# Smaller conversion steps, earlier loads, another order of the second sweep and four more quarters of h loaded ahead, in a retention and mixture-of-experts kernel

## The chip, the cores and the metric

The kernel runs on one core of a Trainium2 chip. The metric is the device time of one execution in microseconds (us). The engines are TensorE (PE in the profile), VectorE (DVE), ScalarE (ACT), GpSimd (POOL) and SyncE (SP), which here only issues DMAs. Each engine works through its instructions in the order in which they were written, and waits for others by semaphores.

## The reference

All tensors are float32. First a retention layer runs over q, k and v of shape (4 batches, 8 heads, 768 positions, 64):

```python
for t in range(S):
    state = gamma * state + einsum('bhd,bhe->bhde', k[:, :, t], v[:, :, t])
    y[:, :, t] = scale * einsum('bhd,bhde->bhe', q[:, :, t], state)
```

Its output, as x of shape (3072 tokens, 512), goes through a mixture of 8 experts with 1024 hidden features, weighted by P, which comes from 8 Sinkhorn iterations:

```python
P = exp(x @ w_gate - max)
for _ in range(8):
    P /= P.sum(1, keepdims=True) + 1e-09
    P /= P.sum(0, keepdims=True) + 1e-09
    P *= N / E
for e in range(E):
    out += P[:, e:e + 1] * (maximum(x @ w1[e], 0) @ w2[e])
```

## The kernel before

**Precision.** PE takes its operands in a reduced float32 form. Every operand is split into a high part (rounded by ACT, `hi_act`, L77) and a low part (the difference, by DVE or POOL, `lo`, L80), and every product is made of three matmuls: high by high, low by high, high by low.

**Seven products.** Both expert layers multiply 2 x 2 blocks with seven products, M1 to M7, instead of eight. This needs sums and differences of blocks: of x (`x_tasks`, L128, through the scratch tile XSC), of w1 (`w1_tasks`, POOL adds at L158), of h, and of w2. A tile of x, `X0` or `X1`, has seven operands, each with a high slot and a low slot of 1024 columns; `XP` says which operand stands where.

**Attention.** 24 turns `tau`, each a chunk of 128 positions of one batch. In a turn: `loads(tau + 3)` puts the raw q, k and v of a later chunk on SP's queue; `split_qk(tau + 2)` makes high and low parts (kh, QH on ACT, kl on POOL, QL on DVE); `scores(tau + 1)`, `logits(tau - 1)`, `attend(tau)` and `state` work on PE, with evictions on DVE, and POOL scales keys (tk) and decays the state. `attend` stores the chunk of x to `xd` in HBM. From turn 8 on, tasks in the list `todo` are run two to a turn: the 22 steps that make X0 for the first third of the tokens (r = 0), and the conversion of the first two blocks of w1.

**First layer (UA).** 96 units, one for each pair of a block j of w1 (32 blocks of 256 hidden features) and a third r of the tokens. A unit is seven products of six matmuls each. `ROW` sets the order of seven groups: group m = 0 is M6 of unit n, m = 1 is M1 of unit n + 1, then M3 and M7 of n, M2 and M5 of n + 1, and M4 of n. `post` evicts each product by ACT or DVE, and SP stores seven parts of h to `hd`. M1, M6, M7 and M4 accumulate one upon the other in a PSUM bank, M5 and M3 in another, so a product waits for the eviction of the one before it. `order` sets which unit follows which: units 0 to 31 are all blocks with r = 0 (the first sweep); then r = 1 and r = 2 (the second sweep), in which a block is used for both. A job is one conversion of a block; three buffers `WA` hold converted blocks, and the raw tile `RW` holds two raw blocks. r = 0 and r = 2 use X0, r = 1 uses X1. Between groups, `run(wq, 1)` starts one task of w1, and `run(xq, ...)` one or two steps of x. At the end of units 12 to 30 one step of Sinkhorn (`sink`) follows.

**Second layer (UB).** 24 units, one for each pair of an expert and a third of the tokens, of 28 parts each. A part `s` is a quarter of one product, 6 matmuls. The raw quarter of h (later its low part) lies at `place(s)`, the high part in the ring `HH`. Quarters are loaded by `h_load` into a ring `HL` of 15 places in the three WA buffers, as these come free at the end of the first layer; quarters 8 to 11 lie in the slots of M1 in X0 instead (`HX`). `h_conv` makes high and low parts, five parts ahead. The first parts are worked in between the groups of the last unit of the first layer, the rest after it.

## Time and profile before

| what | value |
|---|---|
| median of 3 runs | 2055.17 us (2054.22 to 2057.34) |
| profiled execution | 2053.89 us |
| its span in the trace | 2051.8 us |
| mean granted clock of PE in it | 0.987 |
| PE busy | 1985.9 us, 97% of the span |
| DVE busy | 1527.7 us, 74% |
| ACT busy | 1041.7 us, 51% |
| POOL busy | 406.0 us, 20% |
| moved by DMA | 504.13 MB, 246 GB/s on average |

The profile is one execution, by the hardware profiler. A row of the timeline has the start and the duration in us, the engine, the line of the kernel, the operation, what it writes and reads, a count, and in brackets the idle time of the engine before it with what ended it. Matmul ends are modelled, so start times are the better measure for PE. A row of the busy times by stage gives, for a stretch of the span, its length, the busy time of each engine with its number of instructions, the clock granted to PE (1.00 is full), the busy share of the DMA engines and GB/s. A row of groups gives line, engine, operation and shapes, count, busy time and mean ns of one, and the idle time before with its main releasers.

### The profile page before, as it was taken

What the parts mean: (1) busy time and instruction counts of PE and PEld (TensorE: products, weight loads), DVE (VectorE), ACT (ScalarE), POOL (GpSimd) and SP (SyncE); (2) the same over time, 40 slices, a digit from 0 to 9 for tenths busy, and PEclk for the clock granted to TensorE, in tenths of its full rate; (3) what the DMA queues carried; (4) which work ended last, traced back from release to release, by engine and by line L of the source; (5) the groups of instructions that cost most, each with busy time, mean ns of one, the idle gap of its engine ahead of it and who ended that gap; (6) DMA issues with size and microseconds to landing.
All of it is one profiled execution on the core that took longest, in us unless ns stands there. A gap on an engine that the chain in (4) does not pass through costs nothing.

```text
span 2051.8 us, 28824 instructions
## 1 busy us (share of the span) xinstructions
PE 1985.9 (97%) x9273; PEld 1647.2 (80%) x9273; DVE 1527.7 (74%) x2083; ACT 1041.7 (51%) x1668; POOL 406.0 (20%) x422
## 2 busy tenths in 40 slices
PE   7797999998899999999999999999999999999998
PEld 7786887887688888888887788888888888888887
DVE  6795988995666666666677787878778777868766
ACT  3343564554444444444444565655555555655553
POOL 5462342341211121121123000100100101001001
PEclk9899999999999999999999999999999999999999
DMA  7755776776466666666667888998999999999997
GB/s 240 239 180 163 242 245 206 244 244 217 165 233 214 218 228 217 221 218 223 220 229 263 297 286 281 278 288 277 285 283 278 267 291 270 291 292 269 271 269 184
DMA packets 253191, 504.13 MB, mean 246 GB/s; under 512 B 27824, under 2 KB 40432, under 8 KB 250992
## 3 DMA queue, kind: packets, MB, share of 16 engines
q1 hardware_dynamic: 241088, 458.78, 66.3%
q0 software_dynamic: 11952, 43.52, 11.0%
q8 instruction: 72, 1.18, 0.2%
q14 instruction: 79, 0.65, 0.1%
HBM read 269.31 MB, written 232.88 MB: 245 GB/s over the span
## 4 chain that ended last, share of the span: by engine, by line
PE 90%; DVE 4%; DMA 3%; issue 1%; ACT 1%; SPq 1%; POOL 0%; DVEq 0%; ACTq 0%
PE psA L190 42%; PE psA L551 25%; PE psB L551 19%; DMA raw<-kT 1%; DVE QL L80 1%; PE ps_s L327 1%; PE ps_x L363 1%; DMA RW<-w 1%; PE psA L372 1%; PE ps_x L358 0%; PE ps_t L339 0%; DVE X L80 0%; DVE ta L330 0%; SPq L112 0%; DMA hd<-OT 0%
## 5 line engine op out<-in xcount | busy, mean ns | idle before, releaser
L190 PE MATMUL psA<-X,WA 128*128 128x512 f32 x4032 | 931.4, 393 | 24.1 <-DVE OT L213 18.8
L190 PEld LDWEIGHTS psA<-X,WA 128*128 128x128 f32 x4032 | 760.8, 189 | 190.2 <-DVE OT L213 20.9
L77 ACT ACTIVATE WA<-WA 128x512 fp32r<-128x512 f32 x668 | 403.1, 629 | 259.3 <-PE psB L551 116.7
L551 PE MATMUL psA<-WA,X 128*128 128x512 f32 x2296 | 531.4, 389 | 0.2 <-DVE XSC L562 0.2
L551 PEld LDWEIGHTS psA<-WA,X 128*128 128x128 f32 x2296 | 431.0, 188 | 89.9 <-issue 0.6
L551 PE MATMUL psB<-WA,X 128*128 128x512 f32 x1728 | 404.3, 390 | 5.1 <-ACT WA L77 3.1
L80 DVE TENSOR_TENSOR WA<-WA,WA 128x512 fp32r<-128x512 f32 x487 | 313.7, 685 | 99.4 <-ACT WA L77 94.9
L551 PEld LDWEIGHTS psB<-WA,X 128*128 128x128 f32 x1728 | 324.6, 188 | 74.8 <-ACT WA L77 4.2
L158 POOL TENSOR_TENSOR RW<-RW 128x256 f32<-128x256 f32 x244 | 220.8, 915 | 637.9 <-DMA RW<-w 412.8
L219 ACT ACTIVATE OT<-OT 128x512 f32<-128x512 f32 x96 | 60.7, 632 | 243.3 <-DVE OT L218 243.3
L80 DVE TENSOR_TENSOR WA<-RW,WA 128x768 fp32r<-128x768 f32 x122 | 142.5, 1169 | 54.0 <-ACT WA L77 53.9
L569 POOL DMA_DIRECT2D out<-XSC x56 | 48.5, 865 | 611.7 <-DVE XSC L564 365.6
L80 DVE TENSOR_TENSOR WA<-WA 128x512 fp32r<-128x512 f32 x181 | 121.7, 697 | 35.4 <-ACT WA L77 34.4
L213 DVE TENSOR_TENSOR OT<-psA,OT 128x512 f32<-128x512 f32 x96 | 66.2, 689 | 106.2 <-PE psA L190 106.2
L77 ACT ACTIVATE WA<-RW 128x768 fp32r<-128x768 f32 x122 | 109.4, 946 | 23.6 <-POOL RW L158 13.9
L225 DVE TENSOR_TENSOR OT<-psA,OT 128x512 f32<-128x512 f32 x96 | 66.2, 690 | 58.5 <-ACT OT L219 51.3
L229 ACT ACTIVATE OT<-psA 128x512 f32<-128x512 f32 x96 | 57.5, 599 | 77.1 <-PE psA L190 40.3
L236 DVE TENSOR_TENSOR OT<-OT 128x512 f32<-128x512 f32 x96 | 92.2, 961 | 3.3
L579 ACT ACTIVATE OT<-psA 128x512 f32<-128x512 f32 x96 | 57.4, 598 | 72.7 <-PE psA L551 68.8
L226 ACT ACTIVATE OT<-OT 128x512 f32<-128x512 f32 x96 | 60.7, 633 | 65.4 <-DVE OT L225 65.3
L240 DVE TENSOR_TENSOR OT<-OT 128x512 f32<-128x512 f32 x96 | 70.1, 730 | 30.0 <-ACT OT L229 26.1
L211 ACT ACTIVATE OT<-psA 128x512 f32<-128x512 f32 x96 | 57.4, 598 | 64.0 <-PE psA L190 63.9
(116 smaller groups left out, 1486.4 us busy)
## 6 DMA issues: line engine op xcount, KB each, us to landing
hd<-OT SPq DMA_DIRECT2D x672, 256.0 KB, 2.6
WA<-hd SPq DMA_DIRECT2D x668, 256.0 KB, 6.1
RW<-w SPq DMA_DIRECT2D x61, 512.0 KB, 4.5
out<-XSC POOLq DMA_DIRECT2D x56, 512.0 KB, 8.3
RW<-w SPq DMA_DIRECT2D x16, 1024.0 KB, 7.7
out<-OT POOLq DMA_DIRECT2D x27, 512.0 KB, 8.4
OT<-pd SPq DMA_DIRECT2D x23, 512.0 KB, 6.2
raw<-kT SPq DMA_DIRECT2D x24, 256.0 KB, 4.0
```

Of the source, the lines that this page charges most:

```text
L77: act.activation(o, i, AF.Copy)
L80: eng.tensor_tensor(o, full, rd(h), ALU.subtract)
L158: eng_add.tensor_tensor(x[:, WP[o]], x[:, WP[p]], x[:, WP[q]], op)
L190: pe.matmul(ps, w[:, a, k * P:(k + 1) * P], x[:, b, k * 512:(k + 1) * 512], start=i in PRE and k == 0 and m == 0, stop=k == 1 and m == 2, ...
L213: dve.tensor_tensor(c12, ps, u2, ALU.add)
L219: act.activation(o, o, AF.Relu)
L225: dve.tensor_tensor(o, ps, s1, ALU.add)
L226: act.activation(o, o, AF.Relu)
L229: act.activation(self.new("A12"), ps, AF.Relu)
L236: dve.tensor_tensor(t["S2"], t["S1"], t["A11"], ALU.subtract)
L240: dve.tensor_tensor(self.new("S4"), self.t["A12"], self.t["S2"], ALU.subtract)
L551: pe.matmul(ps[d] if isinstance(ps, tuple) else ps[:, d, :], w[:, a, q * 256 + d * P:q * 256 + d * P + P], h[b], start=i in PRE and q == 0 ...
```

## The change

Five things are changed.

1. **Steps of x.** `x_tasks` still has 22 steps, but each now holds one DVE operation (a difference, or a low part) and at most one rounding on ACT, and a low part comes four steps or so after its rounding. Before, a rounding and its low part were one step. The loads of `x_load` can be issued by halves, and come in another order.
2. **Tasks of w1.** The adds on POOL and the roundings on ACT become two tasks, so a job has four tasks, run in groups 0, 3, 5 and 6 (before: three, in groups 0, 1 and 5). Sinkhorn's maximum becomes three steps and its exponential three steps of up to six operations; they run at the ends of units 14 to 35, the last one (the transpose of P) at unit 38.
3. **Earlier loads.** Half of X0's loads are issued at turn 5 of attention, the other half at turn 8, after the loads of w1 jobs 0 and 1, whose tasks now come first in `todo`, in pairs; `todo` starts at turn 10. Jobs 2 and 3 are loaded at turn 16 (before: job 2 after attention, behind the loads of X1). The steps of X1 start in unit 1 instead of 0.
4. **Order of the second sweep.** Before: blocks 29, 30, 31 for r = 1, then for r = 2, then block after block. Now: 29, 30, 31 for r = 1; 28, 27, 26 for r = 1 and then r = 2; 29, 30, 31 again, converted a second time, for r = 2; then block after block. So there are 64 jobs instead of 61, and six units with r = 1 ahead of the first with r = 2. The reload of X0 stays at unit 32, its steps start in unit 33, five to a unit, with one low part in three on POOL.
5. **Quarters of h.** `HX` has eight places, in the slots of M1 and M2 of X0, instead of four. In the last unit of the first layer twelve quarters are loaded instead of eight, after it quarters 16 to 22 instead of 12 to 18.

The diff, without the exponential's operations, which are only put in a list:

```diff
-    def x_load(t, r):
-        for i, c, d in ((M1, 0, 0), (M7, 1, 0), (M3, 1, 1), (M2, 0, 1)):
-            for k in range(2):
+    def x_load(t, r, which=(0, 1)):
+        for i, c, d in ((M1, 0, 0), (M2, 0, 1), (M7, 1, 0), (M3, 1, 1)):
+            for k in range(2) if c in which else ():
...
     def x_tasks(t, engs):
...
-            tt(M5, b12, src(M1))
-            tt(M6, src(M3), src(M5))
-            tt(M7, src(M3), b12)
-            tt(M4, src(M2), src(M6))
-            for i in (M1, M5, M2, M6, M7, M3, M4):
-                one(i)
+            def step(n, w=w, src=src):
+                b12 = rd(w(M7))
+                hi = [M1, M2, M5, M6, M7, M3, M4][n] if n < 7 else None
+                if n < 4:
+                    o, a, b = [(M5, b12, src(M1)), (M6, src(M3), src(M5)), (M7, src(M3), b12), (M4, src(M2), src(M6))][n]
+                    dve.tensor_tensor(XSC[:, sc[o], :], a, b, ALU.subtract)
+                else:
+                    i = [M1, M5, M2, M6, M7, M3, M4][n - 4]
+                    lo(engs[n % len(engs)], w(i, 1), src(i), w(i, 0))
+                if hi is not None:
+                    hi_act(w(hi, 0), src(hi))
+
+            q += [lambda n=n, step=step: step(n) for n in range(11)]
...
             tt(M7, M1, M7, ALU.subtract)
+
+        def rounded():
             hi_act(a[:, 0:3, 0, :], x[:, 0:3, :])
             hi_act(a[:, 3:7, 0, :], x[:, 3:7, :])
...
-        return [adds, lambda: rest(slice(0, 3)), lambda: rest(slice(3, 7))]
+        return [adds, rounded, lambda: rest(slice(0, 3)), lambda: rest(slice(3, 7))]
...
-    for g in [[NJ - 3, NJ - 2, NJ - 1]] + [[j] for j in range(NJ - 4, 2, -1)] + [[2, 1, 0]]:
-        order += [(j if j >= NJ - 3 else 2 * NJ - 4 - j, j, r) for r in (1, 2) for j in g]
+    order += [(j, j, 1) for j in (NJ - 3, NJ - 2, NJ - 1)]
+    order += [(NJ + k, NJ - 4 - k, r) for r in (1, 2) for k in range(3)]
+    order += [(NJ + 3 + k, NJ - 3 + k, 2) for k in range(3)]
+    for g in [[j] for j in range(NJ - 7, 2, -1)] + [[2, 1, 0]]:
+        order += [(2 * NJ - 1 - j, j, r) for r in (1, 2) for j in g]
...
+                if tau == B + 1:
+                    x_load(X0, 0, (0,))
                 if tau == 2 * B:
-                    x_load(X0, 0)
                     w1_load(0)
                     w1_load(1)
-                    todo += x_tasks(X0, [dve]) + w1_tasks(0, pool, dve) + w1_tasks(1, pool, dve)
-                if tau > 2 * B:
+                    todo += [f for g in zip(w1_tasks(0, pool, dve), w1_tasks(1, pool, dve)) for f in g]
+                    x_load(X0, 0, (1,))
+                    todo += x_tasks(X0, [dve])
+                if tau > 2 * B + 1:
                     run(todo, 2)
+                if tau == 4 * B:
+                    w1_load(2)
+                    w1_load(3)
...
-        sink = [sink_max, sink_exp] + [sink_a, sink_b] * SINKHORN + [sink_t]
+        sop = sink_exp()
+        sink = [sink_max, sink_max2, sink_max3]
+        sink += [lambda k=k: run(sop, 6) for k in range(3)]
+        sink += [sink_a, sink_b] * SINKHORN + [sink_t]
...
-        HX = [X0[:, XP[M1], k // 2, (k % 2) * 512:(k % 2 + 1) * 512] for k in range(4)]
+        HX = [X0[:, XP[i], k // 2, (k % 2) * 512:(k % 2 + 1) * 512] for i in (M1, M2) for k in range(4)]
 
         def place(s):
-            return HX[s - 8] if 8 <= s < 12 else HL[(s if s < 8 else s - 4) % NHL]
+            return HX[s - 8] if 8 <= s < 16 else HL[(s if s < 8 else s - 8) % NHL]
...
         x_load(X1, 1)
-        wq = []
-        xq = x_tasks(X1, [dve])
-        w1_load(2)
+        wq, xq = [], []
         loaded = conv = 2
...
-        loaded = 3
+        loaded = 4
...
+            if n == 1:
+                xq = x_tasks(X1, [dve])
             if n == NJ:
                 x_load(X0, 2)
-                xq = x_tasks(X0, [dve, pool])
+            if n == NJ + 1:
+                xq = x_tasks(X0, [dve, dve, pool])
...
-                for s in (range(4) if n == NUA - 2 else range(4, 12)):
+                for s in (range(4) if n == NUA - 2 else range(4, 16)):
...
-                if m in (0, 1, 5):
+                if m in (0, 3, 5, 6):
                     run(wq, 1)
-                if m in (1, 6) or n >= NJ:
-                    run(xq, 2 if n >= NJ else 1)
+                if m in (1, 6) or n >= NJ and m in (0, 3, 5):
+                    run(xq, 1)
...
-            if 12 <= n < 12 + len(sink):
-                sink[n - 12]()
+            if 14 <= n < 13 + len(sink):
+                sink[n - 14]()
+            if n == 38:
+                sink[-1]()
...
-        for s in range(12, NHL + 4):
+        for s in range(16, NHL + 8):
             h_load(s)
```

More of the change, by code (lines that the diff above doesn't have):

```diff
@@ L117, in x_tasks @@
         sc = {M7: 0, M5: 1, M6: 2, M4: 3}
-        e = [engs[k % len(engs)] for k in range(22)]
         for k in range(2):
@@ L459, in sink_exp @@
             dve.tensor_copy(mx, ps[:, 0:1])
+        def sink_exp():
             x, n, r, q = [et[:, i, :] for i in range(4)]
             s1, s2 = [ei[:, i, :].bitcast(mybir.dt.int32) for i in range(2)]
[L462 to L466 removed]
@@ L475, in sink_exp @@
-            p2 = Pm.rearrange("p a b -> p (a b)")
-            dve.scalar_tensor_tensor(q, q, 1.0, s1.bitcast(F32), ALU.add, ALU.mult)
-            dve.tensor_tensor(p2, q, s2.bitcast(F32), ALU.mult)
+            l2, p2 = [t.rearrange("p a b -> p (a b)") for t in (L, Pm)]
+            ops = [
+                lambda: dve.tensor_scalar(x, l2, mx, -104.0, ALU.subtract, ALU.max),
+                lambda: dve.tensor_scalar(n, x, LOG2E, MAGIC, ALU.mult, ALU.add),
+                lambda: dve.tensor_scalar(n, n, MAGIC, None, ALU.subtract),
+                lambda: dve.scalar_tensor_tensor(r, n, -LN2_HI, x, ALU.mult, ALU.add),
+                lambda: dve.scalar_tensor_tensor(r, n, -LN2_LO, r, ALU.mult, ALU.add),
+                lambda: dve.tensor_scalar(x, n, -126.0, None, ALU.max),
+                lambda: dve.tensor_tensor(n, n, x, ALU.subtract),
+                lambda: dve.tensor_scalar(s1, x, 127.0, 8388608.0, ALU.add, ALU.mult),
+                lambda: dve.tensor_scalar(s2, n, 127.0, 8388608.0, ALU.add, ALU.mult),
+                lambda: dve.tensor_scalar(q, r, EXPC[0], None, ALU.mult),
+            ]
@@ L479, in sink_a @@
+            ops += [lambda c=c: dve.scalar_tensor_tensor(q, q, c, r, ALU.add, ALU.mult) for c in EXPC[1:]]
+            ops += [
+                lambda: dve.scalar_tensor_tensor(q, q, 1.0, s1.bitcast(F32), ALU.add, ALU.mult),
+                lambda: dve.tensor_tensor(p2, q, s2.bitcast(F32), ALU.mult),
+            ]
+            return ops
         def sink_a():
```

32 lines of the change are left out of this document (5 added, 27 removed).

## The prediction

> **What bounds the kernel now.** I read the page's busy shares first, then the chain of waits, then the busy time by stage, and last PE's timeline where a stage is not dense.
>
> ```profile
> span 2051.8 us, 28824 instructions
> PE 1985.9 (97%) x9273; PEld 1647.2 (80%) x9273; DVE 1527.7 (74%) x2083; ACT 1041.7 (51%) x1668; POOL 406.0 (20%) x422
> ```
> ```profile
> 537.53 571.94 PE psA L190 x2520
> ...
> 1142.38 5.44 PE psA L551 x24
> ```
>
> PE sets the end, so only time in which PE stands still, or runs at half clock, can be won. The chain gives the dense price: 571.94 / 2520 = 0.227 us for one matmul of 512 columns, 42 x 0.227 = 9.53 us for one unit of the first layer; 5.44 / 24 is the same price in the second layer. The stages by windows:
>
> ```profile
> core 0: us, PE busy (x) PEld busy (x) DVE busy (x) ACT busy (x) POOL busy (x), PEclk, DMA share, GB/s
> 63.70:96.20 32.50, 22.22 (x175) 20.92 (x173) 18.58 (x29) 8.83 (x16) 12.00 (x10) 0.74 0.73 235
> 96.20:166.30 70.10, 63.05 (x572) 57.47 (x571) 63.54 (x92) 25.59 (x41) 38.29 (x32) 0.95 0.51 163
> 166.30:222.20 55.90, 47.73 (x192) 37.69 (x192) 35.16 (x43) 23.95 (x39) 19.02 (x20) 0.94 0.65 207
> ...
> 332.70:500.30 167.60, 167.60 (x741) 138.37 (x740) 141.27 (x216) 86.49 (x136) 50.98 (x56) 0.99 0.71 234
> ...
> 507.00:537.50 30.50, 18.09 (x60) 13.21 (x60) 22.39 (x24) 12.59 (x24) 15.96 (x11) 0.83 0.39 125
> 537.50:1109.50 572.00, 571.96 (x2521) 472.58 (x2521) 369.03 (x482) 267.94 (x425) 110.65 (x122) 1.00 0.64 222
> 1109.50:1136.40 26.90, 21.77 (x85) 16.30 (x85) 21.43 (x23) 12.45 (x23) 12.52 (x8) 0.94 0.97 324
> 1136.40:2045.00 908.60, 908.40 (x4005) 751.85 (x4006) 708.89 (x981) 517.92 (x829) 71.74 (x83) 1.00 0.92 276
> ```
>
> From 537.5 to 1109.5 and from 1136.4 to 2045 PE is full at clock 1.00: nothing is to be had there. What is loose lies in five places: 63.7 to 166.3 (attention), 166.3 to 222.2 (start of the first sweep), around 310 to 330 (the first Sinkhorn steps), 507 to 537.5 (start of the second sweep over x) and 1109.5 to 1136.4 (the change of layers). PE's timeline names the waits:
>
> ```profile
> 166.28 11.18 PE L190 MATMUL psA<-X,WA 128*128 128x512 f32 x48 [0.45 <-DVE L L435]
> 182.96 11.15 PE L190 MATMUL psA<-X,WA 128*128 128x512 f32 x42 [5.50 <-DVE OT L213]
> 196.47 25.47 PE L190 MATMUL psA<-X,WA 128*128 128x512 f32 x102 [2.35 <-DVE OT L213]
> 222.25 85.43 PE L190 MATMUL psA<-X,WA 128*128 128x512 f32 x372 [0.31 <-ACT OT L229]
> 309.89 0.27 PE L453 MATMUL pmx<-ident,mx 128*1 128x128 f32 x1 [2.22 <-DVE mx L451]
> ...
> 329.98 15.38 PE L190 MATMUL psA<-X,WA 128*128 128x512 f32 x54 [2.88 <-DVE OT L213]
> ...
> 512.89 6.25 PE L190 MATMUL psA<-X,WA 128*128 128x512 f32 x18 [5.89 <-DVE OT L213]
> 521.70 5.73 PE L190 MATMUL psA<-X,WA 128*128 128x512 f32 x24 [2.55 <-ACT OT L229]
> ```
>
> **Part 1, start of the first sweep.** From 166.28 to 222.25 there are 48 + 42 + 102 = 192 matmuls, 43.6 us dense, in 56.0 us: 12.4 us are lost. PE names DVE L213, an eviction, but what DVE and ACT were held by is the raw W:
>
> ```profile
> 178.79 0.84 ACT L77 ACTIVATE WA<-RW 128x768 fp32r<-128x768 f32 x1 [6.14 <-DMA RW<-w]
> ...
> 192.85 0.85 ACT L77 ACTIVATE WA<-RW 128x768 fp32r<-128x768 f32 x1 [3.48 <-DMA RW<-w]
> ```
>
> Jobs 2 and 3 of W are loaded only after attention, job 2 behind the eight loads of X1 on SP. The change issues both at turn 16 of attention, eight turns ahead, and lets later jobs follow a unit earlier; it also moves X1's steps from unit 0 to unit 1. Both waits (5.50 and 2.35) and what the lower clock (0.94) took with them should go. The adds on POOL and the rounding on ACT become separate tasks, so ACT no longer stands behind POOL. I keep 2 us for a first unit that is not smooth: gain 10.5, bounds 7.8 (the two waits alone) to 12.4.
>
> **Part 2, first Sinkhorn steps.** The maximum, its transpose and 17 exponent steps now come in six units instead of two, at most 6 small DVE operations each, and each PE step finds its DVE operand a unit old. The waits of 2.22 and 2.88 go: gain 5, bounds 2.2 (only the transpose) to 7 (with the tails of both).
>
> **Part 3, start of the second sweep over x.** From 507 to 537.5 PE does 60 matmuls, 13.6 us dense: 16.9 us lost. X0 cannot be reloaded before its last use, and then 22 steps run at two to a matmul group while DVE waits for the loads with evictions behind it:
>
> ```profile
> 511.00 1.23 DVE L128 TENSOR_TENSOR XSC<-X,XSC 128x512 f32<-128x512 f32 x1 [1.66 <-DMA X<-xd]
> ```
>
> Six units on X1 now stand in front of the first on the new X0 instead of three, the steps begin one unit after the load and come at five a unit, ending in unit 37 before that unit's second group needs them. What is late next is DVE. Its base is the row of 332.7 to 500.3: 141.27 / 167.6 x 9.53 = 8.0 us a unit, W conversion and Sinkhorn included (they now reach to unit 35). Units 33, 34 and 35 add 5, 3 and 5 DVE operations of the x steps (the other two lo steps of unit 34 are POOL's); the price of one:
>
> ```profile
> 187.57 0.68 DVE L128 TENSOR_TENSOR XSC<-X,XSC 128x512 f32<-128x512 f32 x1
> ...
> 192.96 8.04 POOL L158 TENSOR_TENSOR RW<-RW 128x256 f32<-128x256 f32 x8 [10.07 <-DMA RW<-w]
> ...
> 194.60 1.21 DVE L128 TENSOR_TENSOR XSC<-X 128x512 f32<-128x512 f32 x1
> ```
>
> The same operation takes 0.68 us alone and 1.21 us while POOL adds. At 0.68, DVE needs 11.4, 10.0 and 11.4 us against 9.53: 4.2 us too much. At 1.21 it needs 14.0, 11.6 and 14.0: 11 us too much. Evictions queue behind these steps, and PE waits for evictions. I take 4 us, nearer the first, as POOL's four adds fill under half a unit and evictions that read PSUM are in the base already: gain 13, bounds 16.9 - 11 = 6 to 16.9.
>
> The Trainium skill, SBUF — State Buffer, "SBUF: two separate sides", says that a DVE operation with two SBUF inputs and a POOL operation that reads SBUF exclude each other for a whole instruction. The rows of 0.68 and 1.21 agree in direction, and by the rule taken strictly the second price would hold for every step that meets POOL; this is rival A.
>
> Three more W jobs are the price of the new order (29 to 31 come a second time).
>
> ```profile
> L158 POOL TENSOR_TENSOR RW<-RW 128x256 f32<-128x256 f32 x244 | 220.8, 915 | 637.9 <-DMA RW<-w 412.8
> ...
> L80 DVE TENSOR_TENSOR WA<-RW,WA 128x768 fp32r<-128x768 f32 x122 | 142.5, 1169 | 54.0 <-ACT WA L77 53.9
> ```
>
> Each is four POOL adds (3.7 us), two rounds on ACT, two DVE operations (2.3 us) and one 512 KB load. They fall in units 39 to 41, in the stage where DVE is busy 369 of 572 us and DMA 0.64: hidden, 0. Without that cover they would cost 3 x 2.3 = 7 us.
>
> **Part 4, attention.** At turn 8, SP issues eight loads of X0 and two of W ahead of the next raw loads:
>
> ```profile
> 63.70 6.97 SPq L112 DMA_DIRECT2D X<-xd  x8
> 65.53 1.14 PE L358 MATMUL ps_x<-raw,st 128*128 128x128 f32 x8
> ...
> 70.71 1.20 SPq L152 DMA_DIRECT2D RW<-w  x2
> 70.84 1.14 PE L358 MATMUL ps_x<-raw,st 128*128 128x128 f32 x8
> ...
> 79.54 0.63 ACT L77 ACTIVATE kh<-raw 128x512 fp32r<-128x512 f32 x1 [14.61 <-DMA raw<-kT]
> ...
> 84.37 0.55 PE L327 MATMUL ps_s<-QH,kh 128*128 128x256 f32 x1 [10.28 <-DVE ta L330]
> 88.63 2.05 PE L358 MATMUL ps_x<-raw,st 128*128 128x128 f32 x8
> ```
>
> A turn is 70.84 - 65.53 = 5.31 us; the next took 17.8: 12.5 us lost, 10.28 idle and the rest at half clock (2.05 against 1.14 for the same eight matmuls). The change issues four of the eight loads at turn 5. SP's block at turn 8 falls from 8.2 to 1.2 + 3.5 = 4.7 us, with 1 MB less in the queue: the wait shrinks by 3.5 to 6; I take 5. Turn 5 gets a block of 3.5 us of its own, which holds the raw loads behind it and through them kh and the scores; some slack takes most: cost 0 to 3.5, I take 1. The two W loads at turn 16 block SP for 1.2 us: cost 1.
>
> The adds of W jobs 0 and 1 move from turns 20 and 21 to turn 10, both at once:
>
> ```profile
> 144.86 4.14 POOL L158 TENSOR_TENSOR RW<-RW 128x256 f32<-128x256 f32 x4
> ```
>
> That is 8.3 us on POOL, with kl, tk and the decay of the state queued behind, then the scores. Cost 0 to 8.3; since turn 10 stands in the remaining wait of turn 8 anyway, I take 2, and 2 back where they were. X0's steps move from turns 9 to 19 to turns 14 to 23, where the last four have no state update: gain 2 of the 63.54 / 70.10 DVE load. Net 5 - 1 - 1 - 2 + 2 + 2 = 5, bounds -4 to +10.
>
> The Trainium skill, TensorE: Matmul & The Clock Gate, "What's actually happening", halves the clock after an idle window of about 3.4 us. By it the shrunken wait of about 5 us still costs a cold start, so the half-clock part of turn 8 stays; my 5 has not counted it as won.
>
> **Part 5, change of layers.** Four more quarters of h go into the place of M2 in X0, loaded in the last unit instead of after it.
>
> ```profile
> 1124.00 3.40 SPq L620 DMA_DIRECT2D X<-hd  x4
> ...
> 1131.81 2.92 PE L551 MATMUL psB<-WA,X 128*128 128x512 f32 x6 [2.92 <-ACT WA L77]
> ```
>
> The waits of this stage (2.92) are for the conversion of quarters 0 to 3, whose place and load do not move; DVE is busy 21.4 of 26.9 us. The first quarters that come earlier are 12 to 15, used after 1142, and there PE is dense already. The four issues put 3.4 us on SP ahead of the last unit's stores, for which only later units wait. I take 0, bounds -3.4 to +2.9.
>
> **Sum.** 10.5 + 5 + 13 + 5 + 0 = 33.5. The profiled execution took 2053.89 us (2.1 outside its span), 1.3 below the median 2055.17, so 2053.9 - 33.5 = 2020.4 there, and about 2021.5 as a median. Changes under 0.2% (4 us) can't be told from none.
>
> **Rivals.** A: DVE bounds units 33 to 35 at the contended price, 11 us instead of 4: 2028.5. For it: the 1.21 row; against: POOL works 4 of 9.5 us. B: attention wins nothing or loses, because POOL's 8.3 us at turn 10 and SP's block at turn 5 each make a stall with a cold clock: -4 instead of +5, 2030.5. For it: POOL has 38.3 of 70.1 us taken already; against: the adds fall into a wait. C: the earlier quarters relieve the change of layers: 2.9 more, 2018.5; against it, the quarters waited for are others. D, slower than before: the split tasks put both lo steps of a W job at the end of a unit (groups 5 and 6, before: 1 and 5), and the next unit's second group needs the first of them. If DVE is late there, each of 62 conversions stalls PE. From 33.5 / 62 = 0.54 us a job the whole gain is eaten; at 0.7 us the time is 2021.5 + 43 = 2065. Against it: with DVE at 8.0 of 9.53 us a unit the operation should end a group (1.36 us) ahead. E: the loads are not earlier in fact, because SP reaches them late: 2050 to 2055.
>
> **Chances.** Forecast 0.64 (own range 2012 to 2028), A 0.13, B 0.12, C 0.05, D 0.03, E 0.03. A with B would be 2037, C with the better ends of parts 1 to 4 about 2010; that is the range. Slower holds D alone, 0.03; within 0.2% about 0.02 of E; faster 0.95.
>
> **What would show it.** Right: no wait over 1 us before an L190 matmul in the first 60 us of the sweep, none at the transpose of the maximum, the second x sweep without a gap beyond 4 us in units 32 to 38, a wait of about 5 us at turn 8, and the change of layers as before. Wrong: a stall at turn 10 or 11 behind POOL L158 (B), DVE without idle time and PE waits <-DVE L213 at units 33 to 35 (A), short waits on DVE WA L80 in every unit (D).

## The result, and the profile after

| | before | after |
|---|---|---|
| median us | 2055.16 (2054.22 to 2057.34, 4 runs) | 2041.35 (2039.92 to 2043.97, 4 runs) |
| ratio to before | 1 | 0.9933, 95% interval 0.9918 to 0.9947 |
| profiled execution, its span | 2053.89, 2051.8 | 2039.92, 2037.7 |

The changed kernel is 13.8 us faster, where 33.5 was forecast: outside the range, which began at 2010 and ended at 2037. The head of its page:

```profile
span 2037.7 us, 28903 instructions
PE 1987.3 (98%) x9273; PEld 1645.8 (81%) x9273; DVE 1547.5 (76%) x2096; ACT 1039.5 (51%) x1674; POOL 433.7 (21%) x427
```

The number of matmuls is the same (9273). DVE is busy 19.8 us longer and POOL 27.7. Part of it is the three added conversions; on DVE part is also seven operations of the second x that POOL made before; the rest is the same operations taking longer. The busy times by stage of the changed kernel; the columns are those of the prediction's view. The stages are attention from turn 4 on, units 0 and 1 of the first layer, units 2 to 31, 32 to 38, 39 to 92, 93 to 95, and the second layer:

```profile
core 0: us, PE busy (x) PEld busy (x) DVE busy (x) ACT busy (x) POOL busy (x), PEclk, DMA share, GB/s
41.50:174.80 133.30, 111.35 (x986) 103.20 (x985) 105.46 (x152) 42.92 (x70) 75.40 (x65) 0.91 0.61 197
174.80:198.50 23.70, 23.66 (x104) 19.59 (x105) 13.85 (x20) 11.92 (x19) 3.14 (x4) 1.00 0.74 222
198.50:493.90 295.40, 293.93 (x1275) 235.71 (x1273) 270.76 (x354) 155.29 (x249) 116.52 (x109) 1.00 0.71 236
493.90:569.20 75.30, 70.45 (x301) 56.39 (x299) 61.59 (x93) 36.82 (x62) 22.56 (x20) 0.98 0.71 228
569.20:1084.40 515.20, 514.85 (x2271) 425.70 (x2272) 332.70 (x437) 240.29 (x384) 112.06 (x116) 1.00 0.65 224
1084.40:1122.60 38.20, 34.41 (x134) 26.50 (x133) 30.29 (x34) 20.05 (x36) 15.07 (x10) 0.91 0.86 302
1122.60:2037.70 915.10, 908.79 (x4009) 751.83 (x4007) 710.88 (x984) 517.59 (x828) 71.73 (x83) 1.00 0.92 274
```

A unit is taken to end where the eviction of A12 starts (line 229 before, 225 after). With the same marks in the trace of before, the ledger is:

| stage | before us | after us | gain | forecast |
|---|---|---|---|---|
| up to the first matmul of the first layer | 166.3 | 174.8 | -8.6 | +5 (Part 4) |
| units 0 and 1 | 35.3 | 23.7 | +11.6 | +10.5 (Part 1) |
| units 2 to 31 | 298.6 | 295.4 | +3.2 | +5 (Part 2) |
| units 32 to 38 | 83.9 | 75.3 | +8.6 | +13 (Part 3) |
| units 39 to 92 | 514.5 | 515.2 | -0.7 | 0 (Part 3) |
| units 93 to 95, second layer | 953.2 | 953.3 | -0.1 | 0 (Part 5) |

The gains add to 14.0 of the 14.1 us by which the span fell. The start of the sweep came as forecast, and the change of layers did nothing. Attention became slower instead of faster, and that alone is 13.6 of the 19.4 us that are missing.

PE's timeline shows where the waits stand now. The row of 174.84 runs on through 655 matmuls, and neither the 5.50 and 2.35 us of the first units nor the 2.22 and 2.88 us around the first Sinkhorn steps are left. Waits of 3.23 and 1.09 us stand in units 33 to 35:

```profile
174.84 151.89 PE L186 MATMUL psA<-X,WA 128*128 128x512 f32 x655 [0.45 <-DVE L L440]
...
524.65 14.13 PE L186 MATMUL psA<-X,WA 128*128 128x512 f32 x54 [3.23 <-DVE OT L209]
...
541.48 27.67 PE L186 MATMUL psA<-X,WA 128*128 128x512 f32 x120 [1.09 <-ACT OT L225]
```

**Attention after.** Turn 4 is the first with a state matmul (`ps_x<-raw,st`), and starts of these count the turns. Turn 7, from 58.15 on, took 10.3 us instead of 5.3. SP, ACT, DVE and PE show why, one after the other:

```profile
50.83 2.66 SPq L112 DMA_DIRECT2D X<-xd  x4
53.62 0.54 SPq L283 DMA_DIRECT2D raw<-qT  x1
54.20 0.43 SPq L283 DMA_DIRECT2D raw<-kT  x1
```
```profile
59.96 0.63 ACT L77 ACTIVATE kh<-raw 128x512 fp32r<-128x512 f32 x1 [7.40 <-DMA raw<-kT]
```
```profile
61.15 2.79 DVE L80 TENSOR_TENSOR QL<-raw,QH 64x512 fp32r<-64x512 f32 x2 [4.09 <-ACT QH L77]
63.96 1.29 DVE L329 TENSOR_TENSOR ta<-ps_s,msk 128x512 f32<-128x512 f32 x2
```
```profile
58.15 1.14 PE L357 MATMUL ps_x<-raw,st 128*128 128x128 f32 x8
...
64.80 0.55 PE L326 MATMUL ps_s<-QH,kh 128*128 128x256 f32 x1 [3.40 <-DVE ta L329]
...
68.43 1.14 PE L357 MATMUL ps_x<-raw,st 128*128 128x128 f32 x8
```

The four loads of X0 issued at turn 5 hold SP for 2.66 us, and the raw k behind them, issued at 54.20, is there only for 59.96. ACT's rounding waits for it, DVE's low part of q waits for ACT, and the masked scores (ta), for which PE waits, stand behind that low part on DVE. The scores then run at half clock (0.55 and then 0.41 us, elsewhere 0.36 and 0.28). The block at turn 8 did shrink: the turn that waits for it, turn 10, took 13.2 us instead of 17.8.

Between 104 and 128 us, turns 13 to 15, it is DVE that is late:

```profile
103.69 2.39 DVE L80 TENSOR_TENSOR WA<-RW,WA 128x768 fp32r<-128x768 f32 x2
106.00 2.97 DVE L80 TENSOR_TENSOR QL<-raw,QH 64x512 fp32r<-64x512 f32 x2
109.00 1.29 DVE L329 TENSOR_TENSOR ta<-ps_s,msk 128x512 f32<-128x512 f32 x2
110.20 0.68 DVE L366 TENSOR_TENSOR RX<-ps_x,gq 128x512 f32<-128x512 f32 x1
110.80 0.85 DVE L344 TENSOR_TENSOR st<-ps_t,st 64x256 f32<-64x256 f32 x2
111.68 2.36 DVE L80 TENSOR_TENSOR WA<-RW,WA 128x1024 fp32r<-128x1024 f32 x2
```
```profile
109.84 0.36 PE L326 MATMUL ps_s<-QH,kh 128*128 128x256 f32 x1 [2.44 <-DVE ta L329]
...
117.81 0.36 PE L326 MATMUL ps_s<-QH,kh 128*128 128x256 f32 x1 [2.46 <-DVE ta L329]
...
119.08 0.42 PE L326 MATMUL ps_s<-QL,kh 128*128 128x256 f32 x1
...
121.07 2.05 PE L357 MATMUL ps_x<-raw,st 128*128 128x128 f32 x8
```

From 103.69 to 111.68 DVE has no gap: a turn is 8.0 us of DVE work. The low parts of w1 blocks 0 and 1 (1.2 us each) now fall two to a turn into full turns, where two steps of x of 0.7 to 1.0 us stood before, and the low parts of q (QL) beside them take 2.97 us where none took over 2.13 in these turns before. PE waits 2.44 and 2.46 us, and behind the second wait the clock drops again (2.05 us for the matmuls that take 1.14). The three turns took 7.9, 9.0 and 7.5 us; before, 5.3, 6.1 and 6.0.

The two loads of w1 at turn 16 made the wait of turn 7 once more, by the rows of SP, ACT, DVE and PE there. The raw k behind them was issued at 133.85 and is there only for 139.90; PE waits 2.37 us for the masked scores, half clock follows, and turn 18 takes 8.6 us.

**Units 2 to 31 after.** Before, units 13 and 14, with the first Sinkhorn steps, took 11.9 and 15.7 us; now no unit there takes over 10.6. These two now take 9.6 and 10.1, which is 7.9 us gained, yet the stage gained 3.2: the other 28 units became 4.8 us slower together. Groups of before, then of the changed kernel, in the same stretch from 205 to 470 us:

```profile
L80 DVE TENSOR_TENSOR WA<-RW,WA 128x1024 fp32r<-128x1024 f32 (+1 forms) x52 | 64.4, 1239 | 5.5 <-ACT WA L77 5.5
```
```profile
L80 DVE TENSOR_TENSOR WA<-RW,WA 128x768 fp32r<-128x768 f32 (+1 forms) x54 | 82.8, 1572 | 0.0
```

And the waits of PE's weight loads in the changed kernel in that stretch:

```profile
PEld psA L186 <- DVE WA L80: 7.1, 18, 0.5
PEld psA L186 <- ACT OT L225: 2.3, 5, 0.6
```

A low part of w1 takes 1572 ns instead of 1239, and 18 times PE's weight loads wait up to 0.5 us for one. One such place, on DVE, POOL and PE's weight loads:

```profile
325.41 3.16 DVE L80 TENSOR_TENSOR WA<-RW,WA 128x768 fp32r<-128x768 f32 x2
```
```profile
323.05 4.44 POOL L152 TENSOR_TENSOR RW<-RW 128x256 f32<-128x256 f32 x4 [5.62 <-DMA RW<-w]
```
```profile
326.95 4.18 PEld L186 LDWEIGHTS psA<-X,WA 128*128 128x128 f32 x19 [0.54 <-DVE WA L80]
```

The low parts run beside POOL's adds, and the next weight load waits for the first of them. These are the short waits on DVE WA L80 that the prediction named as the sign of rival D.

### The profile page after: what moved, and what is told of

The parts are those of the page before. It is cut to its first block, busy times and chain, and to the rows that moved or that the text cites. A ratio compares the mean times of both kernels' runs of the same rounds, so it can differ in the third digit from the quotient of the medians.

```text
span 2037.7 us, 28903 instructions
## 1 busy us (share of the span) xinstructions
PE 1987.3 (98%) x9273; PEld 1645.8 (81%) x9273; DVE 1547.5 (76%) x2096; ACT 1039.5 (51%) x1674; POOL 433.7 (21%) x427
## 4 chain that ended last, share of the span: by engine, by line
PE 89%; DVE 5%; DMA 2%; issue 2%; SPq 1%; ACT 1%; POOL 0%; DVEq 0%; ACTq 0%
PE psA L186 41%; PE psA L566 26%; PE psB L566 19%; DVE QL L80 1%; DVE WA L80 1%; PE ps_s L326 1%; DVE OT L230 1%; PE ps_x L362 1%; DMA WA<-hd 1%; PE psA L371 1%; DVE ta L329 1%; PE ps_x L357 1%; PE ps_t L338 1%; DMA raw<-kT 1%; SPq L112 0%
## 5 line engine op out<-in xcount | busy, mean ns | idle before, releaser
L152 POOL TENSOR_TENSOR RW<-RW 128x256 f32<-128x256 f32 x256 | 257.2, 1015 | 627.7 <-DMA RW<-w 463.9
L80 DVE TENSOR_TENSOR WA<-WA,WA 128x512 fp32r<-128x512 f32 x484 | 311.3, 686 | 103.9 <-ACT WA L77 92.3
L215 ACT ACTIVATE OT<-OT 128x512 f32<-128x512 f32 x96 | 60.7, 632 | 287.3 <-DVE OT L214 287.3
L80 DVE TENSOR_TENSOR WA<-RW,WA 128x768 fp32r<-128x768 f32 (+1 forms) x128 | 166.7, 1341 | 0.1
L80 DVE TENSOR_TENSOR WA<-WA 128x512 fp32r<-128x512 f32 x180 | 119.2, 697 | 30.4 <-ACT WA L77 29.9
L77 ACT ACTIVATE WA<-RW 128x768 fp32r<-128x768 f32 (+1 forms) x128 | 114.0, 938 | 2.8 <-POOL RW L152 2.8
L230 DVE SCALAR_TENSOR_TENSOR OT<-OT 128x512 f32<-128x512 f32 x96 | 80.9, 842 | 0.7
```

The source lines that it names most:

```text
L77: act.activation(o, i, AF.Copy)
L80: eng.tensor_tensor(o, full, rd(h), ALU.subtract)
L152: eng_add.tensor_tensor(x[:, WP[o]], x[:, WP[p]], x[:, WP[q]], op)
L215: act.activation(o, o, AF.Relu)
L230: dve.scalar_tensor_tensor(t["S1"], TMP[:, 3, :], 0.0, t["A22"], ALU.max, ALU.add)
```

## The experiments

Three theories were open after the traces. **1**: attention lost by the block of loads at turn 5 and by the low parts of w1 in full turns. **2**: the later low parts of w1 cost some 0.3 us a unit. **3**: DVE is the bound in units 33 to 35. Every experiment is an edit of the changed kernel; the diffs of e11, e10 and e12 are shown against e5, e9 and e10. In the table, the first two stage columns are the starts of PE's last state matmuls of attention and of the last eviction of unit 1, the next two the lengths of stages, all from the profiled execution; the ratios are to the kernel before, run beside them.

| kernel | median us | ratio, 95% interval | span | attention's end at | unit 1's end at | units 2 to 31 | units 32 to 38 |
|---|---|---|---|---|---|---|---|
| before | 2055.16 | 1 | 2051.8 | 161.8 | 201.6 | 298.6 | 83.9 |
| after | 2041.35 | 0.9933 (0.9918 to 0.9947) | 2037.7 | 170.4 | 198.5 | 295.4 | 75.3 |
| e1_attn_before | 2033.17 | 0.9898 (0.9872 to 0.9923) | 2031.0 | 161.9 | 190.7 | 296.1 | 75.1 |
| e2_one_piece | 2039.92 | 0.9925 (0.9901 to 0.9949) | 2038.6 | 169.9 | 197.9 | 295.5 | 75.9 |
| e3_lo_early | 2062.96 | 1.003 (1.0014 to 1.0047) | 2064.8 | 172.3 | 203.4 | 306.4 | 75.0 |
| e4_four_quarters | 2041.16 | 0.9931 (0.9908 to 0.9955) | 2038.7 | 169.5 | 199.0 | 295.8 | 75.6 |
| e5_tasks_before | 2033.45 | 0.9894 (0.9872 to 0.9916) | 2031.3 | 169.4 | 199.1 | 288.5 | 74.4 |
| e6_sink_aside | 2042.38 | 0.994 (0.992 to 0.996) | 2036.9 | 170.1 | 198.2 | 296.1 | 73.1 |
| e7_order_before | 2046.09 | 0.9963 (0.9948 to 0.9978) | 2050.6 | 172.2 | 201.8 | 295.5 | 82.4 |
| e8_spread | 2034.58 | 0.9902 (0.9881 to 0.9924) | 2031.9 | 160.8 | 191.1 | 295.7 | 75.5 |
| e9_all | 2026.36 | 0.987 (0.9851 to 0.9888) | 2025.9 | 163.8 | 197.2 | 288.1 | 72.5 |
| e10_pool_share | 2014.69 | 0.9815 (0.9799 to 0.9832) | 2015.7 | 155.3 | 187.6 | 288.2 | 72.4 |
| e11_lo_late | 2049.51 | 0.9972 (0.995 to 0.9995) | 2047.8 | 177.4 | 208.4 | 294.3 | 75.9 |
| e12_x_on_dve | 2016.30 | 0.9821 (0.9793 to 0.985) | 2008.4 | 152.7 | 180.7 | 288.3 | 70.6 |

**Theory 1: attention.** The first edit puts attention's loads and steps back:

```diff
-                if tau == B + 1:
-                    x_load(X0, 0, (0,))
                 if tau == 2 * B:
+                    x_load(X0, 0)
                     w1_load(0)
                     w1_load(1)
-                    todo += [f for g in zip(w1_tasks(0, pool, dve), w1_tasks(1, pool, dve)) for f in g]
-                    x_load(X0, 0, (1,))
-                    todo += x_tasks(X0, [dve])
-                if tau > 2 * B + 1:
+                    todo += x_tasks(X0, [dve]) + w1_tasks(0, pool, dve) + w1_tasks(1, pool, dve)
+                if tau > 2 * B:
                     run(todo, 2)
```

> The changed kernel, with the attention part as before: all eight loads of X0 at turn 8 ahead of w1 jobs 0 and 1, X0's steps first, the two conversions of w1 last, from turn 9 on. Jobs 2 and 3 of w1 stay at turn 16. In the changed kernel the first matmul of the first layer starts at 174.8 us, before at 166.3. Theory 1 (the new order of attention's tasks and loads costs this time): start near 167 to 168 us and 2041.4 - 7 = 2034 us. Rival (the 8.6 us are chance of PE's half-clock phases, or come from the loads of jobs 2 and 3): start stays near 172 to 175 us, 2040 to 2042 us.

In this kernel the loads of blocks 2 and 3 of w1, still at turn 16, come ahead of the conversion of blocks 0 and 1 and replace their values; the work is the same. Attention ended at 161.9 instead of 170.4, and the median fell by 8.2 us: the changed attention costs about what the ledger says. Of the 8.5 us, 2.0 lie ahead of turn 4, where the programs are the same. Units 0 and 1 keep their gain without the changed attention (28.8 us from attention's end to unit 1's end, 28.1 in the changed kernel).

The second edit loads X0 in one piece at turn 8, behind the two loads of w1:

```diff
-                if tau == B + 1:
-                    x_load(X0, 0, (0,))
                 if tau == 2 * B:
...
-                    x_load(X0, 0, (1,))
+                    x_load(X0, 0)
```

> The changed kernel, with only the eight loads of X0 in one piece again, at turn 8 behind jobs 0 and 1 of w1; the order of the tasks stays new. Turn 8 should fall back from 10.3 to 5.3 us and the turn that waits for turn 8's loads (13.2 us) grow to about 17.8. Theory 1a (a block of SP costs about what it holds, wherever it stands): net 0, 2041 us. Theory 1b (two blocks cost more than one, since each costs a cold clock): 3 to 5 us faster, 2037 us. Rival (halving the block is worth what was predicted, 4 us): slower, 2045 us.

The turn of 10.3 us is gone (5.3), and turn 10, which waits for the block at turn 8, takes 16.8 instead of 13.2. From turn 4 to turn 23 it is 125.1 us, against 128.8 in the changed kernel, 122.4 in e1 and 123.5 before. So the split of X0's loads cost 5.0 and gave back 3.6 in these turns, and nothing of it can be told in the median (2039.92 against 2041.35), as theory 1a had it. The 2.7 us between this kernel and e1 (125.1 against 122.4) would be the price of the tasks of w1 ahead of the steps of x, but they are no more than attention varies by chance. This execution reached turn 4 at 44.8 instead of 41.6 us, with the same program up to there, and that chance part is the limit of all these comparisons. Five kernels with the very attention of the changed one (after, e3, e4, e6, e7) took 128.8 to 131.9 us from turn 4 to 23, and turn 4 began between 38.5 and 41.6 us; e5 and e11, which share one program of attention, took 127.6 and 136.8.

The eighth kernel spreads the loads instead:

```diff
...
-                if tau == B + 1:
-                    x_load(X0, 0, (0,))
-                if tau == 2 * B:
-                    w1_load(0)
-                    w1_load(1)
...
+                one = {5: (M1, 0), 6: (M2, 0), 7: (M1, 1), 8: (M7, 0), 9: (M3, 0), 10: (M2, 1), 11: (M7, 1), 12: (M3, 1)}
+                if tau in one:
+                    x_load(X0, 0, only=one[tau])
+                if tau == 10:
                     todo += x_tasks(X0, [dve])
-                if tau > 2 * B + 1:
-                    run(todo, 2)
-                if tau == 4 * B:
-                    w1_load(2)
-                    w1_load(3)
+                if tau in (13, 14):
+                    w1_load(tau - 13)
+                    todo += w1_tasks(tau - 13, pool, dve)
+                if tau > 10:
+                    run(todo, 3 if tau >= 20 else 2)
+            w1_load(2)
...
         x_load(X1, 1)
+        w1_load(3)
```

> The changed kernel with the attention's loads spread: the eight loads of the first x one in each of turns 5 to 12, jobs 0 and 1 of w1 loaded in turns 13 and 14, the small steps of x two to a turn from turn 11 on and w1's behind them (three to a turn from turn 20 on), job 2 loaded behind the last turn and job 3 behind the loads of the second x. Theory (a block of four loads holds SyncE and the state store behind it, 5 us at turn 5 and 8 at turn 8, and the small steps on VectorE hold turns 13 to 16 by 7): no turn of 10 or 13 us, the first layer starts near 158 us instead of 174.8, and the kernel comes at 2025 to 2028. Rival (each load of a turn holds the state's store by its share, and VectorE sets turns of 6 us from turn 11 on): eight turns of 6 to 7 us, the first layer starts at 168 or later and the kernel comes at 2034 or later.

No turn of 10 or 13 us is left (the longest is 8.7), and the first layer started at 166.1 us instead of 174.8: between the theory's 158 and the rival's 168. The median, 2034.58, is the rival's. From 95 us on DVE sets the pace, as the rival had it. The stretch from 95 to 125 us of this kernel:

```profile
95.00:125.00 30.00, 23.39 (x208) 21.58 (x204) 29.51 (x39) 10.06 (x17) 17.54 (x12) 0.94 0.73 233
```

DVE is busy 29.51 of 30 us. With the blocks gone, DVE's work is what is left of theory 1. And one load a turn is not shown to be better than one block: e1, with all eight loads at once and the steps in the old order, took 122.4 us from turn 4 to 23 against 121.1 here, and its median was 2033.17. This kernel also loads block 2 of w1 only behind the last turn, ahead of the eight loads of X1, and block 3 behind them. PE still had no wait in units 0 and 1 (busy 24.97 of 25.0 us).

**Theory 2: the tasks of w1.** First the low parts were put earlier than in either kernel:

```diff
-                if m in (0, 3, 5, 6):
+                if m in (0, 1, 2, 3):
                     run(wq, 1)
```

> The changed kernel, with the four tasks of a w1 job in groups 0, 1, 2 and 3 of a unit instead of 0, 3, 5 and 6. Units 2 to 31 of the first sweep take 9.85 us each in the changed kernel, 9.53 dense; the chain shows waits for DVE's low parts of w1 (1.50 us each) at the unit's end, where POOL's adds now run too. Theory 2 (low parts late and against POOL): these units fall to about 9.6 us, 7 us less, 2034 us. Rival (the waits are the Sinkhorn steps' small matmuls and evictions): less than 2 us, 2040 us. The units 33 to 35 should change little by either.

Neither answer: units 2 to 31 took 306.4 us, 11.0 more, and units 39 to 92 526.1, 10.9 more. From 205 to 470 us PE's weight loads wait 25 times, now for ACT. In the rows of one unit the second sum, on DVE, ends at 408.60 and the eviction of A12 starts at 408.69; PE's weight loads wait 0.59 us for it:

```profile
PEld psA L186 <- ACT OT L225: 20.5, 25, 1.2
```
```profile
407.49 1.11 DVE L232 TENSOR_TENSOR OT<-OT 128x512 f32<-128x512 f32 x1
```
```profile
408.69 0.60 ACT L225 ACTIVATE OT<-psA 128x512 f32<-128x512 f32 x1 [0.67 <-issue]
```

The low parts themselves were short there (1112 ns in the mean). They stand ahead of two evictions and the sums on DVE, and so, it seems, push these late. That A12 waits for the sum is read from the 0.09 us between the two rows; the profile itself names no releaser. So the place of a low part matters on both sides. Then the tasks as before:

```diff
-        def rounded():
             hi_act(a[:, 0:3, 0, :], x[:, 0:3, :])
...
-        return [adds, rounded, lambda: rest(slice(0, 3)), lambda: rest(slice(3, 7))]
+        return [adds, lambda: rest(slice(0, 3)), lambda: rest(slice(3, 7))]
...
-                if m in (0, 3, 5, 6):
+                if m in (0, 1, 5):
                     run(wq, 1)
```

> The changed kernel with the tasks of w1 cut and placed as in the kernel before: the seven additions on GpSimd and the two roundings on ScalarE one task, the two low parts on VectorE the second and third, in groups 0, 1 and 5 of a unit. Theory (the later low parts now meet GpSimd's additions and end behind the unit's matmuls, about 0.3 us in each unit with a conversion): units 2 to 31 take 9.65 us in the mean instead of 9.85, some 6 us less, and the kernel comes at about 2035. Rival (what the profile showed of the kernel before, ScalarE's roundings held behind the additions, costs more than the later low parts): units 2 to 31 take as long or longer, and the time is 2041 or more. Third: the sum over units does not move and the time stays within 2 us of 2041.

The theory holds: units 2 to 31 took 288.5 us, 9.62 a unit, 6.9 less, and the median is 7.9 lower. Groups and waits of this kernel from 205 to 470 us:

```profile
L80 DVE TENSOR_TENSOR WA<-RW,WA 128x1024 fp32r<-128x1024 f32 (+1 forms) x55 | 71.1, 1293 | 3.4 <-ACT WA L77 2.8
```
```profile
PEld psA L184 <- ACT OT L223: 1.3, 4, 0.6
...
PEld psA L184 <- DVE OT L212: 0.3, 1, 0.3
```

No wait on a low part is left. Which half of the edit did it? The next kernel keeps additions and roundings in one task in group 0 and puts only the low parts late again:

```diff
-                if m in (0, 1, 5):
+                if m in (0, 5, 6):
                     run(wq, 1)
```

> As e5_tasks_before (additions and roundings of w1 one task in group 0), but both low parts late, in groups 5 and 6 as in the changed kernel, instead of 1 and 5. Theory (it is the place of the low parts that costs: just ahead of the next unit's first use, together with the sums and GpSimd's additions): units 2 to 31 take 9.8 us or more in the mean as in the changed kernel, against 9.60 with groups 1 and 5, and the time is 2040. Rival (it is the split of the roundings, which put them into group 3): units 2 to 31 stay at 9.6 to 9.65 and the time at 2034.

Units 2 to 31 took 294.3 us, near the changed kernel's 295.4, and the waits are back:

```profile
PEld psA L184 <- DVE WA L80: 7.9, 19, 0.5
...
PEld psA L184 <- ACT OT L223: 0.5, 2, 0.3
```

So it is the place of the low parts that costs, 5.8 of the 6.9 us, and hardly the split of the roundings. Its median of 2049.51 is more than that explains, and more than the 2040 expected; in its profile attention ended 8 us later than in e5, with the same program, and its ten runs reach from 2039 to 2056.

**Theory 3: DVE in units 33 to 35.** Two edits; first the Sinkhorn steps out of the way:

```diff
-            if 14 <= n < 13 + len(sink):
-                sink[n - 14]()
-            if n == 38:
-                sink[-1]()
+            if 12 <= n < 32:
+                sink[n - 12]()
+            if 36 <= n < 39:
+                sink[n - 16]()
```

> The changed kernel with the Sinkhorn steps moved out of the start of the second sweep: twenty from unit 12 to unit 31, none in units 32 to 35, the last three in units 36 to 38. Theory (in units 33 to 35 VectorE has more work than TensorE, rival A of the prediction, and the steps are part of that work): units 32 to 38 take 72 to 73 us instead of 75.3, units 2 to 12 stay within 0.5 us, and the kernel comes at 2038 to 2039. Rival (the excess is set by the low parts and adds of x alone, or by ScalarE): units 32 to 38 keep 75.3 within 0.7 us and the time stays at 2041.

Units 32 to 38 fell to 73.1 us, where 72 to 73 was expected, and PE's wait in unit 34 from 3.23 to 2.38 us:

```profile
523.68 15.54 PE L186 MATMUL psA<-X,WA 128*128 128x512 f32 x60 [2.38 <-DVE OT L209]
```

The median (2042.38) does not show the 2.2 us: it is less than attention varies. Then the order of the second sweep as before:

```diff
-    order += [(j, j, 1) for j in (NJ - 3, NJ - 2, NJ - 1)]
-    order += [(NJ + k, NJ - 4 - k, r) for r in (1, 2) for k in range(3)]
-    order += [(NJ + 3 + k, NJ - 3 + k, 2) for k in range(3)]
...
+    for g in [[NJ - 3, NJ - 2, NJ - 1]] + [[j] for j in range(NJ - 4, 2, -1)] + [[2, 1, 0]]:
+        order += [(j if j >= NJ - 3 else 2 * NJ - 4 - j, j, r) for r in (1, 2) for j in g]
...
-                if m in (1, 6) or n >= NJ and m in (0, 3, 5):
-                    run(xq, 1)
+                if m in (1, 6) or n >= NJ:
+                    run(xq, 2 if n >= NJ else 1)
```

> The changed kernel with the second sweep's order as before: the last three operands of w1 used twice at once from unit 32 on, 61 of them formed, three units between the load of the second x and its first use, and its small steps two to a group from unit 32 on. Theory (the order is what gained 8.6 us there, and the three added operands cost about 0.7 us later): units 32 to 38 take 83 to 84 us, units 39 to 92 some 0.5 to 1.5 us less than 515.2, and the kernel comes at 2049. Rival (the smaller steps of x gain it, whatever the order): units 32 to 38 take 77 us or less and the kernel comes at 2042.

Units 32 to 38 went back to 82.4 us, and the waits to 6.31 and 2.74. The order, with the steps at five a unit that it allows, gains 7.1 of the 8.6 us; the other 1.5 came with the rest of the change.

```profile
510.63 6.33 PE L186 MATMUL psA<-X,WA 128*128 128x512 f32 x18 [6.31 <-DVE OT L209]
...
525.63 5.49 PE L186 MATMUL psA<-X,WA 128*128 128x512 f32 x12 [2.74 <-DVE OT L209]
```

The three operands that are not formed again should have shown as 0.5 to 1.5 us less in units 39 to 92. These took 517.0, more than 515.2, so that price was not found.

**Part 5** was undone by itself: four places in `HX`, eight quarters loaded in the last unit.

```diff
-        HX = [X0[:, XP[i], k // 2, (k % 2) * 512:(k % 2 + 1) * 512] for i in (M1, M2) for k in range(4)]
+        HX = [X0[:, XP[M1], k // 2, (k % 2) * 512:(k % 2 + 1) * 512] for k in range(4)]
...
-                for s in (range(4) if n == NUA - 2 else range(4, 16)):
+                for s in (range(4) if n == NUA - 2 else range(4, 12)):
...
```

> The changed kernel with four quarters of h in X0 instead of eight, so the fifth part of the change undone. My theory: no effect, the change of layers as long as in the changed kernel (last unit 17.9 us, then 5.4 us for quarters 4 to 7), 2041.4 within 1 us. Rival (the earlier quarters 12 to 15 cover loads at the start of the second layer): a gap after quarter 11 and 2 to 4 us slower, 2044 us.

2041.16 against 2041.35; units 93 to 95 and the second layer took 952.2 us against 953.3. Nothing that can be told from none.

**Together.** The ninth kernel has the edits of e5, e6 and e8 at once.

> The changed kernel with three edits at once: the loads and small steps of attention spread as in e8_spread, the tasks of w1 as before in groups 0, 1 and 5, and the Sinkhorn steps set aside from units 32 to 35 as in e6_sink_aside. Theory (three separate places, their gains add: 6.8 us in attention, 6.9 in units 2 to 31, 2.2 in units 33 to 35): the first layer starts near 166, units 2 to 31 take 9.62 in the mean, units 32 to 38 72 to 73, and the kernel comes at 2024 to 2027. Rival (the gains overlap, since VectorE has the work left somewhere): units 2 to 31 stay at 9.75 or more, or units 32 to 38 at 75, and the time is 2030 or more.

Units 2 to 31 (288.1 us, 9.60 a unit) and 32 to 38 (72.5) came as the theory had them, and so did the median, 2026.36. The first layer started at 170.9 us in this execution, not near 166: it came to turn 4 at 44.3 us, 4.6 later than e8. The tenth gives part of the steps of attention to GpSimd:

```diff
-                    todo += x_tasks(X0, [dve])
+                    todo += x_tasks(X0, [dve, dve, pool])
```

> As e9_all, and in attention one low part of x in three goes to GpSimd instead of VectorE. Theory (with the blocks gone VectorE sets turns 13 to 19, busy 29.5 of 30.0 us there in e8_spread): these seven turns fall from 50 us to about 45, and the kernel is some 4 us faster than e9_all. Rival (a low part on GpSimd holds VectorE about as long as it saves it, or holds up the scaled keys behind it): the turns take as long or longer and the time is within 2 us of e9_all or above.

2014.69, faster by more than the theory said, and faster than both kernels of this case (0.9815 of before). Of the 10.2 us between the two spans, 3.5 lie ahead of turn 4, where the programs are the same; 4.9 lie in turns 4 to 23 (114.6 against 119.5). Of the latter, the seven turns that were named give 2.2 (44.7 against 46.9), and the last three 4.4 (5.5, 6.5 and 3.9 us instead of 5.0, 8.8 and 6.5), of which the last two run in part at half clock in e9; the turns ahead of the seven take 1.6 back. DVE is as busy as before the edit, rows of e9 and then e10:

```profile
95.00:125.00 30.00, 24.69 (x223) 23.04 (x221) 28.87 (x40) 11.91 (x20) 17.22 (x13) 0.94 0.68 222
```
```profile
95.00:125.00 30.00, 24.84 (x240) 22.73 (x239) 28.89 (x40) 11.61 (x20) 21.58 (x17) 1.00 0.76 246
```

The clock in this stretch is 1.00 instead of 0.94 and PE does 240 matmuls instead of 223. From turn 4 to 23 PE is busy 100.7 instead of 105.5 us for the same matmuls, and DVE 106.2 instead of 106.7: the time came from half clock that did not set in, and not from DVE. The next kernel, e12, has the same attention and took 114.4 us at clock 1.00, on another chip; e8 and e9, without the edit, 121.1 and 119.5 at 0.94. That speaks for the edit and against chance, and the intervals of e9 and e10 do not meet; why the clock stayed up is not shown.

The last kernel takes the other direction in units 33 to 37: there no low part goes to GpSimd.

```diff
-                xq = x_tasks(X0, [dve, dve, pool])
+                xq = x_tasks(X0, [dve])
```

> As e10_pool_share, but all fourteen low parts of the second x are VectorE's; none is GpSimd's. In e10_pool_share a low part on VectorE takes 1.75 us while GpSimd makes one, 0.68 otherwise, and TensorE still waits 2.77 us for an eviction in unit 34. Theory (a low part given to GpSimd saves VectorE 0.68 us and costs it about as much on the operation that it meets, so the four that are given away gain nothing): the wait and units 32 to 38 (72.4 us) stay within 0.7 us or shrink by up to 1.5, and the time stays within 2 us of e10_pool_share. Rival (VectorE's count of operations decides): four more on VectorE, 2.7 us, lengthen units 32 to 38 to about 75 and the time by 2 to 3 us.

Units 32 to 38 shrank by 1.8 us, to 70.6, a little more than the theory allowed, and PE's wait from 2.77 to 1.74, although DVE has four operations more. In e10's rows of POOL and DVE one sees what a low part on POOL costs:

```profile
519.07 1.75 POOL L80 TENSOR_TENSOR X<-XSC,X 128x512 fp32r<-128x512 f32 x1 [10.16 <-ACT X L77]
```
```profile
519.58 1.79 DVE L133 TENSOR_TENSOR XSC<-X 128x512 f32<-128x512 f32 x1
521.29 0.68 DVE L133 TENSOR_TENSOR XSC<-X,XSC 128x512 f32<-128x512 f32 x1
```

The operation of DVE that met it took 1.79 us instead of 0.68, and ended only after POOL's did (521.37 against 520.82). The Trainium skill, SBUF — State Buffer, "SBUF: two separate sides", says that the one which starts first holds the shared port for its whole instruction. The two ends agree with that to 0.13 us (520.82 + 0.68 = 521.50). The median, 2016.30, can't be told from e10's.

## Why the prediction was wrong

**Part 1, right.** 11.6 us gained against 10.5 forecast, within its bounds of 7.8 to 12.4. That the loads of jobs 2 and 3 came late was the cause named, and the waits for them are gone; but eight turns ahead is more than is needed, since e8 loads job 2 just ahead of X1 and has no wait in units 0 and 1 either. Most of the 2 us kept for a rough first unit were not needed: units 1 to 13 take 9.4 to 10.1 us.

**Part 4, wrong in sign, and the step that failed.** It was +5 and came out at -8.6. Four terms of its sum:
- *"some slack takes most: cost 0 to 3.5, I take 1"* for the block at turn 5. It cost 5.0 us, above its own bound. There was no slack: the delay of the raw k passed whole through rounding, low part and scores. The bound counted SP's time alone (2.66 us measured), and neither the X0 loads ahead of the raw k in the DMA queues (5.8 us from its issue at 54.20 to its use at 59.96; one load earlier 3.6, from 47.16 to 50.76) nor the half clock that follows the wait. The gain at turn 8, taken as 5, came out at 4.6 (17.8 to 13.2).
- *"The two W loads at turn 16 block SP for 1.2 us: cost 1"* had the same gap. The raw k behind them took 6.1 us from issue to use, and turn 18 shows the wait and the half clock.
- *"I take 2, and 2 back"* for the adds at turn 10 looked at POOL alone, where one wait of 1.05 us (95.52, for tk) is all that shows. What the moved tasks brought to DVE, two low parts of 1.2 us in a turn that is already full, was put at nothing, though the tasks move as a whole. Turns 13 to 15 cost 7.0 us more than before. The turns that were freed at the end gave back less: 5.3 and 5.3 instead of 6.1 and 8.6, and then 8.6 and 7.8 instead of 7.4 and 5.3, with the loads of turn 16, X0's steps and one more half-clock phase in them.
- *"gain 2"* for the later steps of X0 is part of the same turns and isn't there.

The remaining 3.2 us lie ahead of turn 4, where the program is unchanged; turn 4 began between 38.3 and 44.8 us over all these profiles, so they are put down to chance. That leaves about -5.4 for the change itself, near rival B's -4. Rival B had the right mechanism, each stall with a cold clock, but named POOL at turn 10 in place of DVE from turn 13 on, and left out the loads at turn 16.

**Part 2, right mechanism, too small a gain, its neighbour missed.** Both long units became plain, 7.9 us against 5, above the upper bound of 7. But the other units took 4.8 us of it back, because of the new places of the low parts of w1. That is rival D, which had a chance of 0.03 because DVE was at 8.0 of 9.53 us a unit. It came at a fifth of a us a unit, too little to make the kernel slower. That the stage ended near its forecast, 3.2 against 5, is luck: two errors that nearly cancel. The mean of DVE's load hid that its work has an order: in groups 5 and 6 the two low parts follow the two sums, POOL's adds fall into the same 4 us, and the next unit needs the result. e5 and e11 show it.

**Part 3, right mechanism, too small a price.** Units 32 to 38 gained 8.6 instead of 13 us. The order is what gains (e7). DVE is what is late next, as forecast, and the stage is 8.6 us longer than its seven dense units, rather than 4: between the forecast and rival A's 11. PE stands still for 4.9 us of it (75.30 - 70.45); the lower clock behind the waits (0.98 over 75.3 us) took an estimated 1.5 more; the other 2 are not accounted for. The price was taken near 0.68 us a step because POOL's four adds fill under half a unit. In unit 34 it was otherwise:

```profile
515.00:525.00 10.00, 6.36 (x26) 4.74 (x27) 9.90 (x11) 2.92 (x6) 9.69 (x9) 1.00 0.52 186
```

POOL, with the adds of two blocks and two low parts of x, is busy 9.69 of 10 us, and DVE 9.90 for eleven operations. Steps that meet POOL cost 1.2 to 1.8 us, not 0.68, and the low parts given to POOL did not relieve DVE: the stage is 1.8 us longer with them than without (e12). The three added jobs cost 0.7 us at most against 0.

**Part 5, right**: 0 measured, in the changed kernel and by undoing it (e4), and rival C fell with it. Rival E fell too: the loads are earlier, and units 0 and 1 show it.

## What to carry to other kernels

Price a moved step on every engine that it uses, in the turn where it lands, not against an engine's mean load: an engine with 15% idle time can still have none where the order puts the work. A block of loads put ahead of just-in-time loads passed its whole delay on here, and the stall cost the half-clock phase behind it too. Two such blocks were no cheaper than one (e2), and one load a turn is not shown to be cheaper than either (e8 against e1). For a conversion on DVE, look for a place where PE waits for nothing behind it and GpSimd is idle: in units 2 to 31, too early (e3) cost 18 us and too late (e11) 6 against the old places (e5).
